# Unread unit-matrix products in the prologue of a fused attention and mixture-of-experts kernel

## The chip, the cores and the metric

The program runs on one core of one Trainium2 chip. The metric is the device time of one execution in microseconds (us). Engines are named as the profile names them: PE is TensorE (PEld its weight loads), DVE is VectorE, ACT is ScalarE, POOL is GpSimd, SP issues most of the DMAs.

## What is computed

The reference is attention with pooled queries, followed by a gated feed-forward layer and a top-2 mixture of experts. Only the first stage touches the change:

```python
q_pool = q.reshape(B, H, S // 2, 2, D).mean(axis=3)   # B=2, H=8, S=1152, D=64
scores = scale * np.matmul(q_pool, k.transpose(0, 1, 3, 2))
scores = scores - np.max(scores, axis=-1, keepdims=True)
attn = np.exp(scores)
attn = attn / (np.sum(attn, axis=-1, keepdims=True) + 1e-09)
return np.matmul(attn, v)
```

The result goes through RMS norm, silu(x w_gate) * (x w_val) w_out with 1152 tokens, width 512 and inner width 1536, and then through 8 experts of inner width 1024, two per token. The inputs are float32.

## The kernel before, in words

Heads are worked in pairs p (8 of them), h is 0 or 1 within a pair. Everything is placed by hand: instructions run on each engine in the order in which the program issues them (a manual schedule). The waits between engines are not in the code; the tile framework derives them from the tiles that the instructions read and write.

The **prologue** (L323 to L366) prepares pair 0. `load_kq` loads keys and queries; `split_k` and `split_q` split them into a rounded high part and a low part (L106, L108, L114, L121, L123). `kq_trans(p, h, i)` transposes them on PE through `trans` (the transposes are at L135, out<-identr,source in the profile) into a 512-column PSUM tile `tt`, and ACT copies them out as KT and QH (L141); the call with h = 1, i = 3 has one more copy, of a part of QH to QZ, on DVE (L143). Two `tt` tiles take turns in the prologue.

`s1(p, h, c)` makes the raw scores of 128 queries against all 1152 keys: three products of 384 columns (L188) into a tile of three times 512 columns (`s`; columns 384 to 511 of each third stay unused), and one DVE reduction over all three thirds (L193), which gives the negated row maximum. It is written into a column of Ql. The `s` tiles have two buffers. The prologue runs six of these: pair 0, h = 0, c = 0, 1, 2 and then h = 1, c = 0, 1, 2. They are called S1 to S6 here, and their reductions R1 to R6. S3 can only start when the buffer of S1 has been reduced, and so on.

`ql_trans(p, h)` transposes the three finished parts of Ql; each transpose needs the maximum of its own c. ACT copies the result to QlT (L141). After the second of these (`ql_trans(0, 1)`, L358, transposes t0, t1, t2) comes the **score loop** (L425 on): `st_exp` issues four products of 288 columns per step (L202, L203), ACT takes the exponential (L204), and `kq_trans`, `s1`, `ql_trans` of the next pair and the products with V (L229) are placed between the steps by a table of slots. Later come the feed-forward units (L534, L555) and the experts (L1079, L1106).

The unit matrix is built in float32 on POOL (`ident`) and copied by DVE to `identr` (L331), which the transposes use. `pro.close()` at L365 gives the prologue's PSUM tiles back.

Of the kernel before, what the change touches and what calls it, by code (L numbers as in the profile page):

```python
# [9 lines left out]
F32 = mybir.dt.float32  # L10
# [11 lines left out]
def fused_kernel(ctx, tc, q, k, v, w_gate, w_val, w_out, rms_g,  # L22
                 r_gate, r_noise, noise, e_w1, e_w2, out, dbg=None):
    nc = tc.nc
    P = 128
# [11 lines left out]
    pe, dve, act, pool, sp = nc.tensor, nc.vector, nc.scalar, nc.gpsimd, nc.sync  # L37
# [4 lines left out]
    identr = const.tile([P, P], F32R, name="identr")  # L42
# [29 lines left out]
    Ql = [[ab.tile([P, QN[h], P], F32R, name=f"Ql{i}{h}") for h in range(2)] for i in range(3)]  # L72
# [13 lines left out]
    raw, khl, qh2, KT, QhT, QlT, V = {}, {}, {}, {}, {}, {}, {}  # L86
# [17 lines left out]
    def rnd(eng, o, i):  # L104
        if eng is act:
            act.copy(o, i)  # L106
        else:
            eng.tensor_scalar(o, i, 1.0, 1.0, op0=ALU.mult, op1=ALU.mult)  # L108

    def split_k(p, h, e0, e1):  # L110
        kr = raw.pop((p, h))
        khl[p, h] = t = fr.tile([P, KC, 2, D], F32R, name="khl", tag=f"khl{h}", bufs=1)
        rnd(e0, t[:, :, 0, :], kr)
        e1.tensor_tensor(t[:, :, 1, :], kr, t[:, :, 0, :].bitcast(F32), op=ALU.subtract)  # L114

    def split_q(p, h, e0, e1):
        qr = Qraw[h]
        n = QN[h]
        qh2[p, h] = u = fr.tile([P, n, 2, D], F32R, name="qh2", tag=f"qh{h}", bufs=1)
        qs = fr.tile([P, QC, D], F32, name="qs", tag="qs", bufs=1)[:, 0:n]  # L120
        e1.tensor_tensor(qs, qr[:, :, 0:D], qr[:, :, D:], op=ALU.add)  # L121
        rnd(e0, u, qs[:, :, None, :].to_broadcast([P, n, 2, D]))
        e1.tensor_tensor(Ql[p % 3][h][:, :, 0:D], qs, u[:, :, 0, :].bitcast(F32), op=ALU.subtract)  # L123
# [4 lines left out]

    tpool = [pst]

    def trans(srcs, evacs):
        t = tpool[0].tile([P, 512], F32R, name="tt", tag="T")
        tpool.append(tpool.pop(0))
        for i, a in enumerate(srcs):
            pe.transpose(t[:, i * P:(i + 1) * P], a, identr)  # L135
        for eng, o, lo, hi, rows in evacs:
            i = t[0:rows, lo:hi].bitcast(F32)
            if len(o.shape) == 3:
                i = i.rearrange("p (h c) -> p h c", h=2)
            if eng is act:  # L140
                act.copy(o, i)  # L141
            else:
                eng.tensor_copy(o, i)  # L143

    def kq_trans(p, h, i):
        if i == 0:
            KT[p, h] = ab.tile([P, S], F32R, name="KT", tag=f"KT{h}", bufs=NKT[h])
            qt = QH[p % 2].rearrange("p (h c) -> p h c", h=2)
            QhT[p, 0], QhT[p, 1], QhT[p] = qt[:, 0], qt[:, 1], qt
        kt = KT[p, h]  # L150
        kk = khl[p, h].rearrange("p c a d -> p c (a d)")
        qq = qh2[p, h].rearrange("p c a d -> p c (a d)")
        if i < 2:
            o = i * 512
            trans([kk[:, 4 * i + c] for c in range(4)], [(act, kt[:, o:o + 512], 0, 512, P)])
        elif i == 2:
            trans([qq[:, c] for c in range(4)], [(act, QhT[p, h][:, 0:512], 0, 512, P)])
        else:
            ev = [(act, kt[:, 1024:], 0, P, P)]
            if h == 0:  # L160
                trans([kk[:, 8]], ev)
            else:
                trans([kk[:, 8], qq[:, 4]], ev + [(act, QhT[p][:, :, QF:SQ], P, 2 * P, P),
                                                  (dve, QZ[p % 2][:, QR:], P + QR, 2 * P, P)])
# [1 line left out]
    def kt2_copy(p, h):  # L166
        sp.dma_start(KT2[h][p % NKT[h]][0:D, :].bitcast(F32), KT[p, h][0:D, :].bitcast(F32))

    def ql_trans(p, h):
        if (p, 0) not in QlT:  # L170
            qt = ab.tile([P, 2, SQ], F32R, name="QlT", tag="QlT", bufs=2)
            QlT[p, 0], QlT[p, 1], QlT[p] = qt[:, 0], qt[:, 1], qt
        trans([Ql[p % 3][h][:, c] for c in range(3)], [(act, QlT[p, h][:, 0:384], 0, 384, P)])

    def ql_trans2(p):
        t = tpool[0].tile([P, 512], F32R, name="tt", tag="T")
# [3 lines left out]
            pe.transpose(t[:, i * P:(i + 1) * P], a, m)  # L180
        act.copy(QlT[p][:, :, 384:], t.bitcast(F32).rearrange("p (h c) -> p h c", h=2)[:, :, 0:192])

    def s1(p, h, c):
        t = ps[0].tile([P, 3, 512], F32, name="s1", tag="s1", bufs=ps[1])
        for j in range(3):
            ks = slice(j * 384, (j + 1) * 384)
            if c < 4:
                pe.matmul(t[:, j, 0:384], QhT[p, h][:, c * P:(c + 1) * P], KT[p, h][:, ks], start=True, stop=True)  # L188
            else:
                pe.matmul(t[:, j, 0:384], QhT[p, 0][:, QF:QF + P], KT[p, 0][:, ks], start=True, stop=False)  # L190
                pe.matmul(t[:, j, 0:384], QZ[p % 2],
                          KT[p, 1][:, ks], start=False, stop=True)
        dve.tensor_reduce(Ql[p % 3][h][:, c, D:D + 1], t[:, :, 0:384], axis=AX.XY, op=ALU.max, negate=True)  # L193
# [130 lines left out]
    ps = [pro.enter_context(tc.tile_pool(name="psp", bufs=1, space=PSUM)), 2]  # L324
# [4 lines left out]
    zt = xp.tile([P, H * D], F32, name="zt", tag="xT", bufs=6)  # L329
    pool.memset(zt, 0.0)  # L330
    dve.tensor_copy(identr, ident)  # L331
    split_k(0, 0, act, dve)
    split_q(0, 0, act, dve)
    kt2_ones(0)
# [6 lines left out]
    load_kq(1, 1)  # L341
    sp.dma_start(g_bc, bass.AP(tensor=rms_g.tensor, offset=rms_g.offset, ap=[[0, P], [1, H * D]]))
    s1(0, 0, 0)
    kq_trans(0, 1, 0)
    kq_trans(0, 1, 1)
    s1(0, 0, 1)
    kq_trans(0, 1, 2)
    kq_trans(0, 1, 3)
    kt2_copy(0, 1)
    s1(0, 0, 2)  # L350
    split(1, 0)
    kt2_ones(1)
    split(1, 1)
    for c in range(3):
        s1(0, 1, c)
        if c == 0:
            ql_trans(0, 0)
    ql_trans(0, 1)  # L358
    for t, u in zip(QH, QZ):
        dve.memset(t[:, SQ:SQ + QR].bitcast(F32), 0.0)  # L360
        dve.memset(u[:, 0:QR].bitcast(F32), 0.0)
# [8 lines left out]
    srcs = [w_gate, w_val, w_out]  # L370
# [54 lines left out]
    for p in range(NPB):  # L425
# [5 lines left out]
        if p + 1 < NPB:  # L431
            at(S_LD[0], load_v, p + 1)
            for i in range(2, QC):
                at(S_S1A[i], s1, p + 1, 0, i - 2)
                at(S_S1B[i], s1, p + 1, 1, i - 2)
            for i in range(4):
                at(S_KA[i], kq_trans, p + 1, 0, i)
                at(S_KB[i], kq_trans, p + 1, 1, i)
            at(max(S_KA), kt2_copy, p + 1, 0)
            at(max(S_KB), kt2_copy, p + 1, 1)  # L440
            at(S_QA[1], ql_trans, p + 1, 0)
            at(S_QB[1], ql_trans, p + 1, 1)
# [42 lines left out]
        for i in range(NST):  # L485
            g, c = divmod(i, KC)
# [24 lines left out]
    ps = fps.enter_context(tc.tile_pool(name="psf", bufs=1, space=PSUM, reuse_waits="tile"))  # L511
# [962 lines left out]
```

## Time and profile before

| | |
|---|---|
| median of 3 runs | 820.24 us (820.09 to 821.29) |
| the profiled execution, its own time | 819.98 us |
| its span, first to last instruction | 818.2 us |
| mean granted TensorE clock | 0.987 |
| busy share: PE, DVE, ACT, POOL | 96%, 71%, 51%, 34% |

The span and the rows are of the one profiled execution; its own time is 1.78 us more than its span. In the answers of the trace a row of the order of time gives start, duration, engine, line, operation, out<-in, shape and count; the brackets give the engine's idle time before it and what ended it. Rows of several instructions (x3) merge neighbours on one engine, so their duration is from the first start to the last end. A granted clock of 1.00 stands for 2.4 GHz and 0.50 for 1.2 GHz.

### The profile page before, as it was taken

What the parts mean: (1) busy time and instruction counts of PE and PEld (TensorE: products, weight loads), DVE (VectorE), ACT (ScalarE), POOL (GpSimd) and SP (SyncE); (2) the same over time, 40 slices, a digit from 0 to 9 for tenths busy, and PEclk for the clock granted to TensorE, in tenths of its full rate; (3) what the DMA queues carried; (4) which work ended last, traced back from release to release, by engine and by line L of the source; (5) the groups of instructions that cost most, each with busy time, mean ns of one, the idle gap of its engine ahead of it and who ended that gap; (6) DMA issues with size and microseconds to landing.
All of it is one profiled execution on the core that took longest, in us unless ns stands there. A gap on an engine that the chain in (4) does not pass through costs nothing.

```text
span 818.2 us, 14013 instructions
## 1 busy us (share of the span) xinstructions
PE 782.7 (96%) x5282; PEld 677.6 (83%) x5282; DVE 579.8 (71%) x849; ACT 413.8 (51%) x818; POOL 278.1 (34%) x240
## 2 busy tenths in 40 slices
PE   5999999999999899999999999999999999999993
PEld 4877777777776699999999999979989888888992
DVE  6677677688779766765787645697676958687760
ACT  4656556565667444351333242554475656566530
POOL 8457357358514221221132200203142423414421
PEclk9999999999999899999999999999999999999997
DMA  7354232230133112421142016649997969697311
GB/s 215 87 164 128 59 102 73 59 102 16 44 118 104 52 52 68 138 97 59 54 144 64 1 52 206 208 145 363 335 312 236 319 234 345 223 360 250 120 55 44
DMA packets 72940, 118.83 MB, mean 145 GB/s; under 512 B 7582, under 2 KB 37278, under 8 KB 72864
## 3 DMA queue, kind: packets, MB, share of 16 engines
q1 hardware_dynamic: 67504, 101.55, 38.8%
q0 software_dynamic: 5360, 16.31, 5.8%
q8 instruction: 43, 0.70, 0.4%
q14 instruction: 33, 0.27, 0.1%
HBM read 103.66 MB, written 10.77 MB: 140 GB/s over the span
## 4 chain that ended last, share of the span: by engine, by line
PE 53%; DMA 5%; DVE 3%; issue 2%; POOL 2%; ACT 1%; POOLq 0%; DVEq 0%; ACTq 0%
PE gv L534 17%; PE py L1106 11%; PE ph L1079 11%; PE po L555 9%; DMA xg<-XD,gidx 3%; PE ph L1094 1%; PE xt L979 1%; DMA pr<-out_dram,gidx 1%; DVE wz L1012 1%; POOL xg L1028 1%; PE xt L285 0%; PE xt L654 0%; PE lg L663 0%; ACT wz L106 0%; DMA out_dram<-yo,sidx 0%
## 5 line engine op out<-in xcount | busy, mean ns | idle before, releaser
L534 PE MATMUL gv<-XN,ws 128*128 128x256 f32 (+1 forms) x1152 | 167.1, 298 | 0.0
L534 PEld LDWEIGHTS gv<-XN,ws 128*128 128x128 f32 x1152 | 159.1, 190 | 5.8 <-issue 1.8
L1012 DVE TENSOR_TENSOR wz<-raw,wz 128x1024 fp32r<-128x1024 f32 x112 | 133.9, 1222 | 12.3 <-ACT wz L106 10.5
L193 DVE TENSOR_REDUCE Ql<-s 128x1 fp32r<-128x1152 f32 x72 | 97.3, 1355 | 56.7 <-PE s L188 35.1
L1106 PE MATMUL py<-wz,hTT 128*128 128x512 f32 x552 | 134.3, 395 | 0.4 <-DVE hTT L984 0.4
L204 ACT ACTIVATE et<-st 128x288 f32<-128x288 f32 x288 | 103.5, 417 | 41.2 <-PE st L203 38.8
L1106 PEld LDWEIGHTS py<-wz,hTT 128*128 128x128 f32 x552 | 100.7, 188 | 20.8 <-DVE hTT L984 1.3
L106 ACT CAST wz<-raw 128x1024 fp32r<-128x1024 f32 x112 | 113.5, 1046 | 7.9 <-PE py L1106 7.9
L402 POOL TENSOR_TENSOR ws<-wm,ws 128x1024 fp32r<-128x1024 f32 x18 | 43.7, 2430 | 158.9 <-ACT ws L401 110.3
L202 PE MATMUL st<-QH,KT 128*128 128x288 f32 x288 | 91.8, 334 | 2.4 <-ACT et L204 1.0
L1079 PEld LDWEIGHTS ph<-xgT,wz 128*128 128x128 f32 x768 | 92.5, 189 | 0.6
L1079 PE MATMUL ph<-xgT,wz 128*128 128x256 f32 x768 | 92.7, 281 | 0.0
L555 PE MATMUL po<-ws,hT 128*128 128x512 f32 x324 | 82.7, 394 | 0.0
L203 PE MATMUL st<-QlT,KT 128*128 128x288 f32 x288 | 81.6, 297 | 0.0
L229 PE MATMUL av<-et,v 128*64 128x288 f32 x576 | 77.4, 412 | 0.5 <-ACT xT L234 0.5
L202 PEld LDWEIGHTS st<-QH,KT 128*128 128x128 f32 x288 | 54.4, 189 | 21.9 <-issue 12.3
L544 ACT CAST hT<-sl 128x256 fp32r<-128x256 f32 (+1 forms) x48 | 20.8, 434 | 100.5 <-DVE sl L543 100.0
L555 PEld LDWEIGHTS po<-ws,hT 128*128 128x128 f32 x324 | 58.4, 188 | 10.4
L1140 POOL DMA_INDIRECT out_dram<-yo,sidx x23 | 32.7, 1420 | 99.1 <-DVE yo L1139 49.1
L217 DVE TENSOR_TENSOR es<-es,et 128x576 f32<-128x576 f32 x64 | 61.6, 963 | 1.5
L229 PEld LDWEIGHTS av<-et,v 128*64 128x64 f32 x576 | 38.4, 136 | 27.8 <-issue 3.9
L203 PEld LDWEIGHTS st<-QlT,KT 128*128 128x128 f32 x288 | 54.8, 190 | 0.1
(251 smaller groups left out, 1100.3 us busy)
## 6 DMA issues: line engine op xcount, KB each, us to landing
raw<-in_moe_w_dram SPq DMA_DIRECT2D x112, 512.0 KB
wraw<-in_moe_w_gate_dram SPq DMA_DIRECT2D x6, 1024.0 KB
wraw<-in_moe_w_val_dram SPq DMA_DIRECT2D x6, 1024.0 KB
wraw<-in_moe_w_out_dram SPq DMA_DIRECT2D x6, 1024.0 KB
kraw<-in_k_dram SPq DMA_DIRECT2D x16, 288.0 KB
v<-in_v_dram SPq DMA_DIRECT2D x8, 576.0 KB
KT<-KT SPq DMA_DIRECT2D x16, 288.0 KB
Qraw<-in_q_dram SPq DMA_DIRECT2D x16, 256.0 KB
```

The source lines that it names most:

```text
L106: act.copy(o, i)
L193: dve.tensor_reduce(Ql[p % 3][h][:, c, D:D + 1], t[:, :, 0:384], axis=AX.XY, op=ALU.max, negate=True)
L202: pe.matmul(t[:, 0:NG], KT[p, h][:, cs], QhT[p, h][:, n0:n0 + NG], start=True, stop=False)
L203: pe.matmul(t[:, 0:NG], KT2[h][p % NKT[h]][:, cs], QlT[p, h][:, n0:n0 + NG], start=False, stop=True)
L204: act.activation(et[:, h, :], t[:, 0:NG], AF.Exp, scale=SCALE)
L217: eng.tensor_tensor(acc, acc, e, op=ALU.add)
L229: pe.matmul(av[h * D:(h + 1) * D, 0:NG], V[p][:, h, c, :], ET[p, g, c][:, h, :], start=(c == 0), stop=(c == KC - 1))
L534: pe.matmul(t[:, 0:n], w[a][:, d, j * P:(j + 1) * P], XN[hf][b_][:, d, cs], start=(k_ == 0), stop=(k_ == 11))
L555: pe.matmul(pt, HT[f, hf][a][:, j, c0:c0 + P], w[b_][:, j, :], start=(k_ == 0), stop=(k_ == 5))
L1012: eng.tensor_tensor(lo, RAW[u % 2][i], hi.bitcast(F32), op=ALU.subtract)
L1079: pe.matmul(o, w[a][:, d, j * P:j * P + P], XT[u][c][:, d], start=z + d == 0, stop=z == 2 and d == 3)
L1106: pe.matmul(PL[u, "y", k], x[c][:, f0 + d, k * P:k * P + P], w[a][:, d], start=i == 4 and z + d == 0, stop=i == 7 and z == 2 and d == 1)
```

## The change

A helper `warm(n)` issues n products of the unit matrix with itself, 128 columns each, into columns 384 to 511 of the last third of the newest `s` tile. Nobody reads them. Before the first `s1` there is no such tile, so `warm` takes one buffer of the two from the same tag. The helper is called with 24 right after `identr` is written, with 3 after S5, with 3 after S6, and with 4, 9 and 6 after the three transposes of `ql_trans(0, 1)`. They are called W24, W3a, W3b, W4, W9 and W6 here; 49 products in all, each with its weight load. Nothing is taken out or moved.

```diff
-    def trans(srcs, evacs):
+    def trans(srcs, evacs, gap=()):
         t = tpool[0].tile([P, 512], F32R, name="tt", tag="T")
         tpool.append(tpool.pop(0))
         for i, a in enumerate(srcs):
             pe.transpose(t[:, i * P:(i + 1) * P], a, identr)
+            if i < len(gap):
+                warm(gap[i])
...
-    def ql_trans(p, h):
+    def ql_trans(p, h, gap=()):
...
-        trans([Ql[p % 3][h][:, c] for c in range(3)], [(act, QlT[p, h][:, 0:384], 0, 384, P)])
+        trans([Ql[p % 3][h][:, c] for c in range(3)], [(act, QlT[p, h][:, 0:384], 0, 384, P)], gap)
...
+    spare = [None]
+
+    def warm(n):
+
+        if spare[0] is None:
+            spare[0] = ps[0].tile([P, 3, 512], F32, name="s1", tag="s1", bufs=ps[1])
+        for _ in range(n):
+            pe.matmul(spare[0][:, 2, 384:512], identr, identr, start=True, stop=True)
+
     def s1(p, h, c):
-        t = ps[0].tile([P, 3, 512], F32, name="s1", tag="s1", bufs=ps[1])
+        t = spare[0] = ps[0].tile([P, 3, 512], F32, name="s1", tag="s1", bufs=ps[1])
...
     dve.tensor_copy(identr, ident)
+    warm(24)
     split_k(0, 0, act, dve)
...
         s1(0, 1, c)
         if c == 0:
             ql_trans(0, 0)
-    ql_trans(0, 1)
+        else:
+            warm(3)
+    ql_trans(0, 1, (4, 9, 6))
```

## Rows read from the trace of the kernel before

**Rows 1.** Busy time of each engine in the score loop; its columns stand first.
```profile
core 0: us, PE busy (x) PEld busy (x) DVE busy (x) ACT busy (x) POOL busy (x), PEclk, DMA share, GB/s
23.00:275.00 252.00, 248.09 (x1785) 189.49 (x1784) 195.90 (x217) 155.33 (x419) 127.71 (x105) 1.00 0.30 85
```

**Rows 2.** Order of time, PE, ACT and DVE, from the unit matrix to S3.
```profile
2.09 0.31 DVE L331 CAST identr<-ident 128x128 fp32r<-128x128 f32 x1
5.27 1.25 PE L135 MATMUL tt<-identr,khl 128*128 128x128 f32 x8 [5.27 <-DVE khl L114]
8.17 1.33 PE L188 MATMUL s<-KT,QH 128*128 128x384 f32 x3 [0.55 <-ACT QH L141]
10.00 1.09 ACT L141 CAST KT<-tt 128x512 fp32r<-128x512 f32 x2 [0.41 <-PE tt L135]
11.35 0.67 PE L135 MATMUL tt<-identr,qh 128*128 128x128 f32 x4
11.82 0.33 PE L135 MATMUL tt<-identr,khl 128*128 128x128 f32 x1
12.06 0.59 ACT L141 CAST QH<-tt 128x512 fp32r<-128x512 f32 x1 [0.97 <-PE tt L135]
```

**Rows 3.** Order of time, DVE and PE, from R3 to the score loop.
```profile
13.15 5.14 DVE L193 TENSOR_REDUCE Ql<-s 128x1 fp32r<-128x1152 f32 x4
14.67 0.76 PE L188 MATMUL s<-KT,QH 128*128 128x384 f32 x3
15.82 0.80 PE L188 MATMUL s<-KT,QH 128*128 128x384 f32 x3 [0.39 <-DVE Ql L193]
18.35 0.28 PE L135 MATMUL tt<-identr,Ql 128*128 128x128 f32 x1 [0.99 <-DVE Ql L193]
19.20 0.47 PE L202 MATMUL st<-QH,KT 128*128 128x288 f32 x1 [0.57 <-ACT QlT L141]
```

**Rows 4.** Order of time, ACT in the first steps of the score loop.
```profile
19.95 0.89 ACT L204 ACTIVATE et<-st 128x288 f32<-128x288 f32 x2 [0.80 <-PE st L203]
22.46 0.89 ACT L204 ACTIVATE et<-st 128x288 f32<-128x288 f32 x2 [0.98 <-PE st L203]
23.25 0.58 ACT L141 CAST QH<-tt 128x512 fp32r<-128x512 f32 x1
```

**Rows 5.** Busy time by stretch, columns as in group 1.
```profile
4.00:6.00 2.00, 0.73 (x6) 0.73 (x6) 1.09 (x2) 0.84 (x2) 1.12 (x2) 1.00 0.98 301
18.00:20.00 2.00, 1.08 (x5) 0.94 (x6) 2.00 (x7) 0.53 (x2) 2.00 (x2) 0.85 0.17 60
20.00:22.00 2.00, 2.00 (x11) 1.99 (x11) 0.13 (x2) 1.36 (x3) 1.66 (x3) 0.50 0.78 211
22.00:24.00 2.00, 1.92 (x14) 1.67 (x13) 1.34 (x1) 1.47 (x4) 0.00 (x0) 0.80 0.71 174
```

**Rows 6.** Order of time, PE, later in the score loop.
```profile
30.96 0.45 PE L135 MATMUL tt<-identr,qh 128*128 128x128 f32 x4
36.34 0.22 PE L135 MATMUL tt<-identr,khl 128*128 128x128 f32 x1
```

**Rows 7.** The instructions of L143, and its first one with its neighbours in time.
```profile
L143 DVEq EVENT_SEMAPHORE  x8: 21/21/21, 12.3 to 226.1; - x8
L143 DVE CAST QZ<-tt x8: 214/215/226, 13.0 to 227.2; 128x64 fp32r<-128x64 f32 x8
...
12.70 0.28 ACT L141 CAST QH<-tt 128x128 fp32r<-128x128 f32 x1
13.01 0.23 DVE L143 CAST QZ<-tt 128x64 fp32r<-128x64 f32 x1
```

**Rows 8.** The change from attention to the feed-forward units: stretches, and PE in order.
```profile
275.00:280.00 5.00, 1.52 (x10) 1.28 (x10) 1.03 (x2) 2.67 (x5) 2.35 (x1) 0.88 0.29 118
280.00:285.00 5.00, 4.52 (x22) 4.26 (x22) 4.50 (x12) 1.44 (x4) 0.00 (x0) 0.50 0.01 3
...
279.27 0.90 PE L255 MATMUL xt<-ident,smS 128*128 128x128 f32 x3 [3.48 <-ACT smS L248]
```

## The prediction

> **What bounds the kernel now.** I read the busy time by stretch first, then the order of time from 2 to 24 us, then the granted clock there, then the instructions of L143.
>
> From 23 to 275 us PE is busy 248.09 of 252 us while ACT has 155.33 and DVE 195.90 [rows 1]: the score loop goes at PE's pace, so whatever moves its start or speeds up its first steps moves what follows by as much. The first score product starts at 19.20 [rows 3]; I call that T0.
>
> Up to T0 the order is a chain through three engines. PE starts at 5.27, though `identr` is there at 2.09 + 0.31 = 2.40 [rows 2]. ACT's copies of the second head wait 0.41 and 0.97 us for PE [rows 2]; the last of them ends at 12.70 + 0.28 = 12.98, QZ follows at 13.01 [rows 7], and then DVE runs R3 to R6 without a break, 13.15 to 18.29 [rows 3]. The last transpose, t2, comes 0.06 later at 18.35, and T0 0.85 after that, behind ACT's copy.
>
> PE is slow in two places. The column of the granted clock shows 1.00 at 4 to 6 us and first moves at 18 to 20 [rows 5], but the durations say otherwise: S1 takes 1.33 us [rows 2] and S5, the same three products, 0.76 [rows 3]; four transposes take 0.67 at 11.35 [rows 2] and 0.45 at 30.96 [rows 6]. So the prologue up to about S3 ran at the lower level, 1.2 GHz. The second place is in the rows of the clock: 0.85, 0.50, 0.80 [rows 5]. With a level of 0.50 these means put the fall at about 19.4 (0.6 us of two at half) and the rise at about 22.8. Before that fall PE had only S6 and three transposes in 3.4 us (15.82 to 19.20). The first steps of the score loop therefore run at half speed, and ACT waits 0.80 and 0.98 us there for PE [rows 4].
>
> **The price of one product.** No row shows a unit-matrix product; the nearest are the transposes of 128 columns, with a weight load each. At the lower level four less one is (0.67 - 0.33) / 3 = 0.113 us apiece [rows 2], at the higher one (0.45 - 0.22) / 3 = 0.077 [rows 6].
>
> **Step 1, W24.** It can run from 2.40 and lasts 24 x 0.113 = 2.7 us, to 5.1; the transposes are ready at 5.27. Price 0. If weight loads and columns overlap less than in the transposes it delays them by some tenths, which I keep in the range.
>
> **Step 2, the prologue at the higher level sooner.** W24 and the transposes behind it keep PE at work without a break from 2.40 on, where before it began at 5.27 and had waits until the level rose. ACT's two waits for PE, 0.41 + 0.97 = 1.38 us, bound the gain at R3, because the rest of ACT's chain is its own work. Ends: 0 (the level rises no earlier) and -1.38. I take -1.0, nearer the second, since the work begins 2.9 us earlier but the moment of the rise isn't in any row.
>
> **Step 3, the wait that the change adds.** W3a writes into the third of the `s` tile that R5 reads, though into other columns, and it stands behind R5 in the program. Does it wait for R5? L143 is the row to judge by. The QZ copy only reads `tt`, which PE wrote, and ACT's copies read the same tile. Nothing is overwritten, yet each of the 8 copies has a semaphore instruction of its own (at 12.3, when PE's transposes were through) and the copy itself starts only at 13.01, 0.03 after ACT's copy ended at 12.98 [rows 7]: two waits, one for PE, one for ACT. So accesses of two engines to one PSUM tile are put in order even where no data pass between them. I take it that W3a waits for R5, and that W3b waits for R6. The Trainium skill, page "PSUM — Partial Sum Buffer", section "PSUM bank collisions raise a hardware error", says that accesses of different engines are to be kept apart by bank and quadrant and not by address. By that rule the products must wait too, and the sum would be the one below; without it, that of the first rival.
>
> What is queued behind: PE takes its products in order, so S6 stands behind W3a. Before, S6 started at 15.82, while R5 ran, and R6 followed R5 at once [rows 3]. Now R6 starts after R5's end plus 3 products plus S6: 3 x 0.077 + 0.76 = 0.99 us later at the higher level, 3 x 0.113 + 1.33 = 1.67 at the lower. I take 1.0, as S6 ran at the higher level before.
>
> W3b then waits for R6, and t0 and t1, which were done between the reductions, stand behind it. After R6 PE must issue W3b, t0, W4, t1 and W9 before t2: 3 + 1 + 4 + 1 + 9 = 18 instructions, where it issued t2 alone. That is 18 x 0.077 = 1.39 or 18 x 0.113 = 2.03 us. I take 1.7, between the two: from the end of S5 to the end of R6 PE has only W3a and S6, hardly more than it had before the fall at 19.4, over a longer stretch. The level may fall before this burst or within it. W6 takes 6 x 0.113 = 0.7 at most beside the 0.85 from t2 to T0, in which ACT copies: price 0, and without that copy it would cost 0.5 to 0.7.
>
> **Step 4, the first steps of the score loop.** The burst stands right ahead of T0, so PE enters the loop after dense work. At the higher level ACT's waits of 0.80 and 0.98 [rows 4] shrink to what two pairs of products need, about 0.45 of the first; so 1.3 us is gained at the end of the QH copy (23.25 + 0.58 = 23.83). Half of the 3.4 us at the lower level, 1.7, is the upper end; 0.4 the lower, if the level rises only after the burst and part of the loop. I take -1.1.
>
> **Sum**: -1.0 + 1.0 + 1.7 - 1.1 = +0.6 us. The profiled run took 819.98, 0.26 under the median of 820.24; against the median that gives **820.8**. SP and POOL get nothing new, and no other wait is added: the rest of the loop, DMAs included, shifts with T0.
>
> A second fall of the level lies far behind, at the end of attention: PE idles 3.48 us for ACT and the clock reads 0.88 and 0.50 [rows 8]. The change only shifts it in time; I price it 0, with some tenths either way from run to run, like the 1.2 us between the three times shown.
>
> **Rivals.**
> *The products don't wait.* Then they fill PE's idle time between R4, R5 and R6, PE stays at the higher level, and steps 2 and 4 are left: -1.0 - 1.1 = -2.1 to -1.38 - 1.3 = -2.7, so about 817.8. For it: other columns are written than are read. Against it: L143's second wait. Chance 0.07.
> *The level falls before R5 ends*, in the empty stretch that the wait makes. Then S6 and the burst run at the lower level and part of the loop too: -1.0 + 1.67 + 2.03 - 0.4 = +2.3, 822.5, slower than before. It decides between the end of S5 and the end of R5, some 2 us; for it, the fall before after as little work, against it, that the work before that is denser than it was. Chance 0.18.
> *W24 does not bring the rise forward* (the change doesn't do what it says): step 2 is 0 and the rest stays, +1.6, 821.8. For it: transposes and S1 from 5.27 on did not bring the rise before S3 either. Against it: they had gaps. Chance 0.12.
>
> **How the numbers follow.** My forecast, waits behind R5 and R6 with the level up for the larger part, has 0.63. 0.2% of 820.24 is 1.6 us, about what a measurement of this kernel tells from no change: faster is under 818.6, slower over 821.9. Faster: nearly all of the first rival and 0.04 of the forecast with its good ends together (-1.38 + 0.99 + 1.39 - 1.4 = -0.4, less a favourable shift at the end of attention), 0.10. Slower: 0.14 of the second rival, 0.05 of the third, 0.05 of the forecast, 0.24. Same: 0.66. The range reaches from 818.9, the good ends less the spread of single runs, to 822.4, just short of the second rival's full price (all bad ends together, 0 + 1.67 + 2.03 - 0.4 = +3.3, are left out); about 0.1 lies below and 0.1 above.
>
> **What would show it.** PE's products from about 2.4 us on, and S1 in about 0.76 instead of 1.33 (step 2); R3 near 12.1. The first product after S5 released by DVE's reduction, and a gap on DVE of about 1 us between R5 and R6 (step 3): if R6 follows R5 at once, the first rival holds. t0, t1, t2 all after R6, T0 near 20.9. A granted clock of 1.00 from 20 to 24 us (step 4). A clock of 0.50 already at 16 to 18 us would be the second rival, S1 in 1.3 us the third.

## The result, and the profile after

The changed kernel takes 828.77 us against 820.25 for the kernel before, a ratio of 1.011 (95% interval 1.0096 to 1.0124): 8.5 us slower. That is outside the range of 818.9 to 822.4, on the side of the second rival (the level falls in the stretch that the wait makes), but more than three times its size. The profiled execution has a span of 826.3 us, 8.1 more than before.

The order of time of the changed kernel, PE and DVE, from the first product to the score loop (unread products are L192, the products of S1 to S6 L199, their reductions L204, the score products L213):

```profile
2.45 5.38 PE L192 MATMUL s<-identr 128*128 128x128 f32 x24 [2.45 <-DVE identr L342]
7.64 1.22 PE L135 MATMUL tt<-identr,khl 128*128 128x128 f32 x8
10.45 1.33 PE L199 MATMUL s<-KT,QH 128*128 128x384 f32 x3 [0.55 <-ACT QH L143]
15.43 3.88 DVE L204 TENSOR_REDUCE Ql<-s 128x1 fp32r<-128x1152 f32 x3
16.95 0.76 PE L199 MATMUL s<-KT,QH 128*128 128x384 f32 x3
19.36 0.55 PE L192 MATMUL s<-identr 128*128 128x128 f32 x3 [1.65 <-DVE Ql L204]
19.75 0.74 PE L199 MATMUL s<-KT,QH 128*128 128x384 f32 x3
20.52 1.36 DVE L204 TENSOR_REDUCE Ql<-s 128x1 fp32r<-128x1152 f32 x1 [1.22 <-PE s L199]
21.94 0.90 PE L192 MATMUL s<-identr 128*128 128x128 f32 x3 [1.45 <-DVE Ql L204]
23.76 2.14 PE L192 MATMUL s<-identr 128*128 128x128 f32 x9
25.70 0.33 PE L135 MATMUL tt<-identr,Ql 128*128 128x128 f32 x1
25.83 1.50 PE L192 MATMUL s<-identr 128*128 128x128 f32 x6
27.39 0.61 PE L213 MATMUL st<-QH,KT 128*128 128x288 f32 x1
```

Read against [rows 2, 3], the lateness adds up on the way to the first score product:

| place | before | after | added |
|---|---|---|---|
| first transposes of keys, R3 (W24) | 5.27, 13.15 | 7.64, 15.43 | 2.28 at R3 |
| start of R6 (W3a waits for R5, S6 behind it) | 16.93 | 20.52 | 1.31 |
| t2 after the end of R6 (W3b, W4, W9 in between) | 18.35 | 25.70 | 3.76 |
| T0 after t2 (W6 in between) | 19.20 | 27.39 | 0.84 |

The sum is 8.19. R6's start of 16.93 before is the end of DVE's unbroken run, 18.29 [rows 3], less one reduction of 1.36; after, a run of three and the fourth alone stand in two rows with 1.22 us of idle time between them, released by S6.

The granted clock by stretch, same columns as in [rows 5]:

```profile
20.00:22.00 2.00, 0.55 (x4) 0.23 (x2) 1.48 (x4) 0.00 (x0) 1.91 (x3) 0.91 0.30 65
22.00:24.00 2.00, 2.00 (x11) 2.00 (x11) 0.62 (x5) 0.00 (x0) 1.34 (x2) 0.50 0.86 284
30.00:32.00 2.00, 2.00 (x11) 1.98 (x11) 1.36 (x1) 1.09 (x3) 0.00 (x0) 0.53 0.00 0
```

The level falls at about 21.6 (0.91 is 0.36 us of two at half), in the empty stretch ahead of W3b, and rises at about 31.9. The first steps of the score loop still run at 1.2 GHz, as before. The rows of all score products (L202 before, L213 after; count, shortest, median and longest duration in ns, first and last start) show that nearly all of the loss is there at T0 and travels on: the last one starts at 266.7 before and 275.2 after, 8.5 us apart.

```profile
L202 PE MATMUL st<-QH,KT x288: 290/299/470, 19.2 to 266.7; 128*128 128x288 f32 x144
```

```profile
L213 PE MATMUL st<-QH,KT x288: 290/299/609, 27.4 to 275.2; 128*128 128x288 f32 x144
```

Single spans are a poor measure of two microseconds: from the last start of a score product to the end of its span the kernel before takes 818.2 - 266.7 = 551.5 us, and the kernels below take from 817.7 - 268.3 = 549.4 (w24_only) to 820.7 - 267.5 = 553.2 (w16_wide). Below, claims on the prologue therefore rest on T0 and on this last start.

### The profile page after: what moved, and what is told of

Its sections match the earlier page's. It is cut to its first block, busy times and chain, and to the rows that moved or that the text cites. A ratio compares the mean times of both kernels' runs of the same rounds, so it can differ in the third digit from the quotient of the medians.

```text
span 826.3 us, 14113 instructions
## 1 busy us (share of the span) xinstructions
PE 791.8 (96%) x5331; PEld 687.0 (83%) x5331; DVE 578.5 (70%) x849; ACT 413.5 (50%) x818; POOL 278.1 (34%) x240
## 4 chain that ended last, share of the span: by engine, by line
PE 55%; DVE 3%; DMA 2%; ACT 1%; issue 1%; POOL 1%; another core or an unknown queue 1%; POOLq 0%; DVEq 0%; ACTq 0%
PE gv L548 16%; PE py L1120 13%; PE ph L1093 11%; PE po L569 9%; PE ph L1108 3%; PE xt L993 2%; DMA xg<-XD,gidx 1%; DVE wz L1026 1%; DMA out_dram<-yo,sidx 1%; DMA pr<-out_dram,gidx 0%; PE xt L668 0%; POOL ws L416 0%; PE xt L328 0%; ACT sq L301 0%
## 5 line engine op out<-in xcount | busy, mean ns | idle before, releaser
L204 DVE TENSOR_REDUCE Ql<-s 128x1 fp32r<-128x1152 f32 x72 | 97.4, 1355 | 66.0 <-PE s L199 44.0
L213 PE MATMUL st<-QH,KT 128*128 128x288 f32 x288 | 92.1, 335 | 1.9 <-ACT et L215 1.0
L213 PEld LDWEIGHTS st<-QH,KT 128*128 128x128 f32 x288 | 54.6, 190 | 21.4 <-issue 12.3
```

What stands on the lines that cost most here:

```text
L213: pe.matmul(t[:, 0:NG], KT[p, h][:, cs], QhT[p, h][:, n0:n0 + NG], start=True, stop=False)
```

## Experiments

### The 24 alone, and the others alone

The edits of the two kernels, w24_only and then gaps_only, each against the changed kernel:

```diff
-        else:
-            warm(3)
-    ql_trans(0, 1, (4, 9, 6))
+    ql_trans(0, 1)
```

```diff
-    warm(24)
```

> Only the 24 products ahead of the first transposes; the 3, 3, 4, 9 and 6 are left out. Theory A (a 128-column product in this form takes 0.22 us, twice the transposes' 0.113, and the level isn't raised by it): PE's first transposes at 7.6 instead of 5.27, R3 at 15.4, T0 at 21.5, time +2.3 us, about 822.5. Rival (most of the loss comes from the waits and these 24 cost little, since ACT and POOL bound the prologue): under +0.8 us.

> Without the 24, with the 3, 3, 4, 9 and 6. Theory A with the waits: R6 1.3 us later, t2 another 3.8 later, T0 0.8 later, together T0 at 25.1 and time +5.9 us, about 826.1. Rival (the 24 at the start cause the low level at the end, too): the burst runs at the higher level, T0 at about 22.5, +3 us or less.

Measured: the 24 alone (w24_only) 822.03 us, ratio 1.0022 (1.0005 to 1.0038), +1.9 us of 820.13; the others alone (gaps_only) 825.46, ratio 1.0063 (1.0044 to 1.0081), +5.3. PE in the kernel with the 24 alone:

```profile
2.46 5.38 PE L192 MATMUL s<-identr 128*128 128x128 f32 x24 [2.46 <-DVE identr L342]
10.45 1.33 PE L199 MATMUL s<-KT,QH 128*128 128x384 f32 x3 [0.55 <-ACT QH L143]
20.55 0.28 PE L135 MATMUL tt<-identr,Ql 128*128 128x128 f32 x1 [0.98 <-DVE Ql L204]
20.66 0.45 PE L213 MATMUL st<-QH,KT 128*128 128x288 f32 x1
```

PE in the kernel with the others alone:

```profile
17.15 0.55 PE L192 MATMUL s<-identr 128*128 128x128 f32 x3 [1.66 <-DVE Ql L204]
19.72 0.90 PE L192 MATMUL s<-identr 128*128 128x128 f32 x3 [1.45 <-DVE Ql L204]
21.55 2.14 PE L192 MATMUL s<-identr 128*128 128x128 f32 x9
24.92 0.55 PE L213 MATMUL st<-QH,KT 128*128 128x288 f32 x1
```

Both parts lose by themselves, and the larger part is the one with the waits: the last score product starts at 268.3 and 272.7, 1.6 and 6.0 us later than before. Theory A's time held in both. In the first kernel S1 still takes 1.33 us after 5.4 us of products: these 24 did not raise the level. Its T0 was forecast at 21.5 and came at 20.66, because the score loop follows t2 by 0.11 us where it was 0.85 before; more on that below. In the full change W6 stands in that place and hides this gain of 0.74, which is most of why the two parts, 1.5 and 5.7 us at T0, add up to 7.2 and not to 8.19.

### Form and width of the products

Two kernels against the one with the 24 alone, w24_transposes and then w16_wide:

```diff
-            pe.matmul(spare[0][:, 2, 384:512], identr, identr, start=True, stop=True)
+            pe.transpose(spare[0][:, 2, 384:512].bitcast(F32R), identr, identr)
```

```diff
-            pe.matmul(spare[0][:, 2, 384:512], identr, identr, start=True, stop=True)
+            pe.matmul(spare[0][:, 2, 0:384].rearrange("p (a c) -> p a c", a=3), identr,
+                      identr[:, None, :].to_broadcast([P, 3, P]), start=True, stop=True)
-    warm(24)
+    warm(16)
```

> 24 transposes of the unit matrix in place of 24 plain products, the same tile, columns and sources; no others. Theory A (the form sets the price): 0.113 us each, done by 5.2, first transposes of keys at about 5.27, T0 no later than 19.2, time 818.5 to 820.5 according to whether the level rises sooner. Rival B (the same target columns again and again, or the unit matrix as weights, set the price): 0.22 us each, first transposes of keys at 7.6, +2.3 us as with the plain products.

> 16 plain products of 384 columns (the unit matrix three times side by side) in place of the 24 of 128; no others. Both theories: 0.32 us each, done by 7.6, as long as the 24 took. Theory A (the narrow products left PE half idle and therefore did not raise the level): the level rises before S1, S1 takes 0.76 us instead of 1.33, R3 at about 14.4, +1.2 us. Rival C (products of the unit matrix do not raise the level at all, however wide): S1 takes 1.3 us, R3 at 15.4, +2.3 us as with the 24 narrow ones.

PE with 24 transposes:

```profile
2.46 3.28 PE L192 MATMUL s<-identr 128*128 128x128 f32 x24 [2.46 <-DVE identr L342]
8.13 0.79 PE L199 MATMUL s<-KT,QH 128*128 128x384 f32 x3 [0.44 <-ACT QH L143]
17.19 0.57 PE L213 MATMUL st<-QH,KT 128*128 128x288 f32 x1
```

PE with 16 products of 384 columns:

```profile
2.46 5.47 PE L192 MATMUL s<-identr 128*128 128x384 f32 x16 [2.46 <-DVE identr L342]
10.11 0.79 PE L199 MATMUL s<-KT,QH 128*128 128x384 f32 x3 [0.44 <-ACT QH L143]
18.98 0.57 PE L213 MATMUL st<-QH,KT 128*128 128x288 f32 x1
```

As transposes the 24 end at 5.54 (where the transposes of keys begin), 0.128 us apiece, and as wide products they fill the same time as the 24 narrow ones. In both S1 takes 0.79 us: the level had risen. So rivals B and C fall: the form sets the price, the level can rise behind unit-matrix products, and what they are made of matters. Yet the times are level with the kernel before: 819.38, ratio 0.9992 (0.9972 to 1.0011), and 819.98, ratio 0.9982 (0.9963 to 1.0). Of the 2.0 us that the transposes win at T0, 0.9 are lost again in the first steps, which run in a longer stretch at 1.2 GHz; the last score product starts at 265.6, 1.1 earlier than before, which the ratio cannot tell from nothing. With the wide products T0 is 0.2 earlier and the last start, 267.5, is 0.8 later. In the kernel with transposes:

```profile
16.00:18.00 2.00, 1.01 (x5) 0.87 (x4) 1.92 (x7) 0.48 (x1) 1.83 (x4) 0.61 0.96 226
18.00:20.00 2.00, 2.00 (x9) 1.85 (x9) 0.00 (x0) 1.41 (x3) 2.00 (x2) 0.50 0.14 52
22.00:24.00 2.00, 2.00 (x14) 1.98 (x13) 0.00 (x0) 1.85 (x5) 0.00 (x0) 0.68 0.54 128
```

Worked out as before, these rows put the fall at about 16.4 and the rise at about 23.3, against 19.4 and 22.8 in the kernel before.

### The prices by themselves

Against the kernel before:

```diff
     dve.tensor_copy(identr, ident)
+    w0 = ps[0].tile([P, 3, 512], F32R, name="s1", tag="s1", bufs=ps[1])
+    wf = w0.bitcast(F32)
+    for _ in range(6):
+        pe.matmul(wf[:, 2, 384:512], identr, identr, start=True, stop=True)
+    for _ in range(6):
+        pe.matmul(wf[:, 1, 0:256].rearrange("p (a c) -> p a c", a=2), identr,
+                  identr[:, None, :].to_broadcast([P, 2, P]), start=True, stop=True)
+    for z in range(6):
+        pe.matmul(wf[:, z % 2, 384:512], identr, identr, start=True, stop=True)
+    for z in range(6):
+        pe.transpose(w0[:, z % 2, 384:512], identr, identr)
```

> The kernel before with 6 plain products of 128 columns, 6 of 256, 6 of 128 into two PSUM tiles by turns and 6 transposes of 128 columns, all of the unit matrix, ahead of the first transposes of keys; for their prices at the lower level only. Theory A (a plain product of 128 columns occupies PE as long as one of 256): 0.22, 0.22, 0.22 and 0.13 us apiece. Rival B (writing the same columns again and again is what is slow): the third group is at 0.11 to 0.13, the second over 0.3. Rival D (the price goes by the columns and the 0.22 is a fixed cost plus 0.107 per 128 columns): the second group is at 0.32.

The rows of six are whole groups; a row of five is a group without its first product:

```profile
2.45 1.54 PE L335 MATMUL s<-identr 128*128 128x128 f32 x6 [2.45 <-DVE identr L331]
2.72 1.27 PE L335 MATMUL s<-identr 128*128 128x128 f32 x5
3.79 1.59 PE L337 MATMUL s<-identr 128*128 128x256 f32 x6
4.11 1.27 PE L337 MATMUL s<-identr 128*128 128x256 f32 x5
5.18 1.38 PE L340 MATMUL s<-identr 128*128 128x128 f32 x6
5.29 1.27 PE L340 MATMUL s<-identr 128*128 128x128 f32 x5
6.35 0.96 PE L342 MATMUL s<-identr 128*128 128x128 f32 x6
7.11 0.88 PE L135 MATMUL tt<-identr,khl 128*128 128x128 f32 x8
9.55 0.79 PE L188 MATMUL s<-KT,QH 128*128 128x384 f32 x3 [0.44 <-ACT QH L141]
```

From start to start, six of each: 1.34, 1.39, 1.17 and 0.76 us, or 0.223, 0.232, 0.195 and 0.127 apiece. The differences between the first three lie in the first product of each group: the other five take 1.27 us in all three, and from their first start to the start of the next group 1.07, 1.07 and 1.06 us, 0.21 apiece. A plain product of 128 columns costs what one of 256 costs and about 1.7 times a transpose of 128. Rivals B (the same columns again and again) and D explain nothing. The kernel ran once, in 818.92 us, and is used for these prices alone. One more thing can be read from it: its S1, at 9.55, took 0.79 us, so the level had risen behind this mixed group of 24.

### The wait apart from the price

gaps_transposes against gaps_only:

```diff
-            pe.matmul(spare[0][:, 2, 384:512], identr, identr, start=True, stop=True)
+            pe.transpose(spare[0][:, 2, 384:512].bitcast(F32R), identr, identr)
```

gaps_free against the kernel before; the tile of t0, t1, t2 is taken from its pool after S4 and handed to `ql_trans`, and `trans` calls `fill` after its transposes as the change calls `warm`:

```diff
+    def fill(t, n):
+        for _ in range(n):
+            pe.matmul(t[:, 384:512].bitcast(F32), identr, identr, start=True, stop=True)
...
         if c == 0:
             ql_trans(0, 0)
-    ql_trans(0, 1)
+            tq = tbank()
+        if c:
+            fill(tq, 3)
+    ql_trans(0, 1, tq, (4, 9))
```

> The 3, 3, 4, 9 and 6 as transposes of the unit matrix instead of plain products, in the same places and tile; without the 24. Parts price from wait. Theory (the waits for R5 and R6 stay, only the price falls from 0.22 to 0.13 or, at the higher level, 0.08): the first filler still starts right after R5's end, R6 is 1.0 us later than in the kernel before, t2 then comes 1.4 to 2.3 us after R6, T0 at 21.6 to 22.6, time +1.5 to +3 us, 821.7 to 823.2. Rival (the plain products' price was all of the loss): T0 at 19.2, time 820.

> The change's own plain products of 128 columns, 3 after S5, 3 after S6, 4 after t0 and 9 after t1, but into the unused quarter of the tile of t0, t1, t2, which nobody reads before t2; without the 24, and without the 6 after t2 (they would wait for ACT's copy). Parts the wait from the price: the price is that of gaps_only. Theory (the wait is the root: it empties PE behind S5, the level falls there, and the products then run after R6 at the lower level): no wait, R3 to R6 without a break, level up, 0.13 us apiece, T0 at 19.2 to 19.6, time -1 to 0 us against the kernel before. Rival (the price alone): +2 us or more.

The first keeps the waits and lowers the price. PE:

```profile
17.29 0.62 PE L192 MATMUL s<-identr 128*128 128x128 f32 x3 [1.66 <-DVE Ql L204]
17.71 1.29 PE L199 MATMUL s<-KT,QH 128*128 128x384 f32 x3
20.45 0.62 PE L192 MATMUL s<-identr 128*128 128x128 f32 x3 [1.45 <-DVE Ql L204]
23.66 0.60 PE L213 MATMUL st<-QH,KT 128*128 128x288 f32 x1
```

823.17 us, ratio 1.0024 (1.0012 to 1.0037), +1.9 of 821.25, in the forecast; T0 at 23.66 is later than the 21.6 to 22.6 expected, since the level fell before S6, which took 1.29 us. The last score product starts at 269.9, 3.2 us later than before, against 6.0 in gaps_only. So more than half of the loss stays with the cheaper form, behind the waits, and the plain products' higher price made up the rest.

The second keeps the kind of product and the counts (but for the 6) and removes what makes them wait. DVE and PE, in order of time:

```profile
13.35 5.15 DVE L203 TENSOR_REDUCE Ql<-s 128x1 fp32r<-128x1152 f32 x4 [0.16 <-PE s L198]
15.48 0.44 PE L138 MATMUL tt<-identr 128*128 128x128 f32 x3
17.58 1.19 PE L138 MATMUL tt<-identr 128*128 128x128 f32 x9
18.61 0.25 PE L143 MATMUL tt<-identr,Ql 128*128 128x128 f32 x1
19.43 0.40 PE L212 MATMUL st<-QH,KT 128*128 128x288 f32 x1 [0.57 <-ACT QlT L151]
```

The four reductions run without a break, the nine products take 17.58 to 18.61, 0.114 us apiece at the higher level, and T0 is 19.43 instead of 24.92; the granted clock reads 1.00 in every stretch from 12 to 275 us. 818.06 us, ratio 0.9977 (0.9962 to 0.9992), 2.2 us faster than before where at most 1 was expected; the last score product starts at 265.5, 1.2 earlier. The same products, the 6 after t2 apart, lose 5.3 us in one PSUM tile and win in another.

### Versions without the wait

fill_tt against gaps_free:

```diff
-            pe.matmul(t[:, 384:512].bitcast(F32), identr, identr, start=True, stop=True)
+            pe.transpose(t[:, 384:512], identr, identr)
...
-        if c:
-            fill(tq, 3)
-    ql_trans(0, 1, tq, (4, 9))
+        if c == 1:
+            fill(tq, 7)
+    ql_trans(0, 1, tq, (8, 14))
```

front_and_fill against fill_tt; front24_fill has 24 in place of 21, fill_layout 1, and wide8_fill has 8 of the wide products of w16_wide into `w0` instead:

```diff
     dve.tensor_copy(identr, ident)
+    w0 = ps[0].tile([P, 3, 512], F32R, name="s1", tag="s1", bufs=ps[1])
+    for _ in range(21):
+        pe.transpose(w0[:, 2, 384:512], identr, identr)
```

> No 24. Fillers as transposes of the unit matrix into the unused last quarter of the tile that the transposes t0, t1, t2 write anyway: 7 after S5, 8 after t0, 14 after t1. Nothing reads that tile before t2, so theory: no wait for R5 or R6, R3 to R6 without a break, T0 at 19.2; the level does not fall at 19.4, first steps of the score loop at 2.4 GHz, 1.0 to 1.3 us faster, 819.0. Rival (unit-matrix transposes don't hold the level): it falls as before, 820.1.

> 21 transposes of the unit matrix ahead of the first transposes of keys, as wide as the room there, and the fillers of fill_tt. Theory: done by 5.3, S1 in 0.79 us, R3 at 11.8, T0 at 17.2 as in the kernel with 24 transposes, and the level stays up through the first steps: -2.0 - 1.3 = -3.3 us, 816.8. Rival (what is gained at T0 is given back by a later or longer low level): under 1 us, 819 to 820.

> fill_tt with one transpose of the unit matrix into an s tile ahead of everything, so that the s tiles are placed before the tt tile in PSUM. Theory (the first score product waits for ACT's copy of QlT because its tile lies where the tt tile was; with the other order of allocation it lies elsewhere): T0 0.1 us after t2 instead of 0.8, time 0.5 to 0.7 us less than fill_tt. Rival (the early T0 of the kernels with products ahead comes from something else): T0 - t2 stays 0.8.

> fill_tt with 8 plain products of 384 columns ahead of the first transposes of keys, done by 5.1. Theory (wide products bring the rise forward): S1 in 0.79 us, T0 at about 17.3, 2 us less than fill_tt. Rival (2.6 us of them are too few or their moment decides): S1 in 1.33 us as in front_and_fill, T0 at 18.6, 0.6 us less than fill_tt through the layout alone.

> fill_tt with 24 transposes of the unit matrix ahead, as many as in w24_transposes, where the level rose before S1; with 21 of them it did not. Theory (the moment of the rise is a matter of the run): some runs like w24_transposes with T0 at 17.2 and some like front_and_fill with 18.6, so the median lies 0.5 to 2 us under fill_tt. Rival (three more products decide): all runs 2 us under fill_tt.

| kernel | S1, us | T0 | last score product starts | time | ratio to before |
|---|---|---|---|---|---|
| fill_tt | 1.33 | 19.48 | 265.6 | 818.36 | 0.9965 (0.9952 to 0.9978) |
| fill_layout | 1.33 | 18.50 | 264.9 | 817.88 | 0.997 (0.9958 to 0.9982) |
| front_and_fill | 1.33 | 18.66 | 265.1 | 818.89 | 0.9966 (0.9956 to 0.9977) |
| front24_fill | 0.79 | 17.79 | 264.2 | 817.15 | 0.9957 (0.9937 to 0.9978) |
| wide8_fill | 0.79 | 17.08 | 264.3 | 816.62 | 0.9956 (0.994 to 0.9972) |

All five beat both kernels. Their times come from two groups of runs, in which the kernel before had medians of 821.25 (fill_tt, front_and_fill) and 820.26 (the other three), so they are compared by the ratios. The clock in fill_tt, where [rows 5] had 0.50 and 0.80:

```profile
20.00:22.00 2.00, 2.00 (x19) 2.00 (x18) 0.80 (x1) 1.72 (x5) 1.60 (x2) 1.00 0.90 262
22.00:24.00 2.00, 1.86 (x14) 1.63 (x14) 0.56 (x1) 1.99 (x6) 0.00 (x0) 1.00 0.57 114
```

The level holds, T0 itself gains nothing, and 1.1 us are won by the end of attention (266.7 to 265.6), as step 4 of the prediction had priced it. The ratio says 2.9 us; the further 1.8 do not come from any row of the prologue and stay open. In fill_layout T0 follows t2 by 0.09 us, where [rows 3] has 0.85:

```profile
18.41 0.25 PE L143 MATMUL tt<-identr,Ql 128*128 128x128 f32 x1
18.50 0.36 PE L212 MATMUL st<-QH,KT 128*128 128x288 f32 x1
```

T0 follows t2 by 0.08 to 0.17 us in all eight kernels that take an s tile first from the prologue's pool and have nothing between t2 and T0, and by 0.8 in the kernel before, fill_tt and gaps_free, which take a tt tile first, as expected of the layout; the gain against fill_tt (0.7 us at the last score product) is below what the ratios can tell. For wide8_fill the theory held for the rise and T0, but 2 us less than fill_tt was too much: at the end of attention 1.3 are left. front24_fill, whose runs lie between 814.91 and 818.77, has the median that its theory gave, but not the two groups that would show it. In wide8_fill a new wait takes part, for the DMA that copies the second head's keys:

```profile
7.88 0.79 PE L198 MATMUL s<-KT,QH 128*128 128x384 f32 x3 [0.44 <-ACT QH L151]
17.08 0.36 PE L212 MATMUL st<-QH,KT 128*128 128x288 f32 x1
18.63 0.37 PE L213 MATMUL st<-QlT,KT 128*128 128x288 f32 x1 [0.92 <-DMA KT<-KT]
```

The forecast of -3.3 us for front_and_fill failed in its first half: 21 transposes did not raise the level before S1, 24 did in both kernels that had them and 8 wide products in the one. That its ratio still says -2.8 us is luck: fill_tt has -2.9 without the 21, of which 1.8 are unexplained. With one profile of each it stays open whether three more transposes or the moment of the run decide; its rival, which looked for under 1 us, failed too.

## Why the prediction was wrong

**The price of one product** is the step that failed. The prediction took the transposes as the nearest rows, 0.077 to 0.113 us. The product of the change is no transpose; it measured 0.21 to 0.22 at the lower level, the level at which all but W3a of them ran, outside both ends. The row was the nearest by its columns and its sources, and the form, which no row showed, set the price. Bounds from the nearest rows should have been widened for a form that no row has.

**Step 1** (price 0): W24 lasted 5.2 us instead of 2.7, ended 2.4 us after the place where the transposes of keys stood before (7.64 and 5.27) and moved R3 by 2.28. The room was 2.9 us, so nothing else had to go wrong. The prediction had kept some tenths in its range for products that overlap less than transposes.

**Step 2** (-1.0): 0. R3 came later by just W24's overrun and S1 still took 1.33 us: the third rival's condition. The wide and the transposed versions show that the mechanism exists; these products did not set it off, through 5.2 us of them.

**Step 3**: the mechanism was right. W3a and W3b wait for R5 and R6, 1.65 and 1.45 us by the rows, S6 stands behind, t0 and t1 fall behind R6, and gaps_free shows what becomes of it without the wait. The rule of the Trainium skill, page "PSUM — Partial Sum Buffer", section "PSUM bank collisions raise a hardware error", that was cited there agrees with these two waits: other columns of the same tile were no way around. The waits are those that the framework put in; what the chip would do without them no run shows. Two terms were mis-sized. R6 was 1.31 us later instead of 1.0. The burst cost 3.76 instead of 1.7: 16 products at about 0.22 and two transposes. W6, priced 0 beside ACT's copy, ran 1.5 us and added 0.84; at 0.113 it would have fitted into the 0.85 from t2 to T0.

**Step 4** (-1.1): +0.3. The level was low from 21.6 to 31.9, over the whole burst and the first steps. The step's premise, that dense work ahead of T0 has the level up, failed: PE had the burst and W6 from 21.94 to 27.39 without a break, and the level did not rise in them, as it did not in W24. The second rival was right that the level falls in an empty stretch that a wait makes; it named the one before R5's end, and the fall came in the next one, ahead of W3b. It too had the price at 0.113, and so 822.5 for what measured 828.8. The first rival, no wait, is out by the rows of W3a and W3b.

**Sum**: the prologue added 8.19 at T0 and 8.5 by the last score product, the measured 8.5. Of the 7.9 us between the forecast of +0.6 and this, about 4.9 are the price (W24 2.28, the burst 3.76 less the 2.03 that it was to take at the lower level, W6 0.84), 2.7 the level (steps 2 and 4 with 1.0 and 1.4, and 0.3 because the whole burst ran at the lower one), and 0.3 the later R6. The range had left out the prediction's own bad ends together (+3.3), and even these fall short by 5 us. (Its sum of the good ends has 1.4 for step 4, where that step had named 1.7 as the upper end; it plays no part here.) That the rest of the program shifts as it stands, argued from PE's busy time in the score loop [rows 1], held through attention. What lies behind attention varies too much to test it.

## What to carry to other kernels

An instruction that nobody reads still takes its place in an in-order queue: ask what it writes, who reads the same PSUM tile, and what stands behind it, before asking what it costs. Fillers belong into a tile whose reader comes after them in any case; here the unused quarter of the transposes' own tile turned a loss of 5.3 us into a gain. Price an instruction by a row of its own form or measure it first: six instructions of each kind in one kernel tell 0.21 from 0.13.

## What was not expected

- A plain float32r product of 128 columns takes as long as one of 256 (0.21 us at the lower level, by the rows of five), a transpose of 128 columns 0.127.
- 24 plain narrow products in a row did not bring the level up before S1 in either kernel with a profile; 24 transposes, 8 or 16 products of 384 columns and the mixed 24 of the price kernel did. Once it was up, 29 transposes in PE's gaps held it, and so did 19 plain narrow products in gaps_free. What decides was not tried, and each is one profile.
- The order in which tiles are first taken from a PSUM pool moved the first score product by 0.7 us, presumably because it decides whose bank that product's tile inherits. Which bank it was is taken from the wait for ACT's copy (0.57 us, in [rows 3]) and its absence, not read from a row.
- The column of the granted clock shows 1.00 until its first event, also where S1's duration shows the lower level.
